# Attention in front of two expert layers: query blocks taken in pairs, and V kept in one copy

## Chip, cores and metric

One core of a Trainium2 chip runs the whole program. The metric is the device time of one execution in microseconds (us); of several executions the median is given. The engines are TensorE (PE; its weight loads are PEld), VectorE (DVE), ScalarE (ACT), GpSimd (POOL) and SyncE (SP), which here only issues DMAs.

## The reference

Four batches of eight heads, 576 tokens, head size 64, all in f32. q and k are rotated by position (rope), then attention, then a first expert layer that takes the largest of three products, then a second one in which each token goes to one of eight experts:

```
scores = (1 / sqrt(64)) * q_rot @ k_rot^T          # 4 x 8 x 576 x 576
attn   = softmax(scores)
x      = attn @ v                                  # as 2304 tokens x 512
h      = max(x @ w1, x @ w2, x @ w3)               # 512 -> 768
x      = h @ w_out                                 # 768 -> 512
e      = argmax(x @ w_gate); p = softmax(x @ w_gate)[e]
out    = p * (max(x @ W1[e], 0) @ W2[e])           # 512 -> 1024 -> 512
```

## The kernel before

**Numbers.** Most products are made of f16 pieces: each f32 operand is split into a high and a low f16 part (high = scaled value rounded, low = scaled value minus high), and three of the four products of parts are added up. Batch 0 takes its scores in f32 instead.

**Units of attention.** A batch has 36 units, made in `attention`. The tokens 0 to 511 of a batch make four query blocks c of 128 tokens (one tile of the later layers each), the last 64 tokens a fifth one. A unit (c, h) with c < 4 is one head of one query block; a unit (4, u) takes two heads of the last 64 tokens, one on each half of the partitions. The order is a list: all eight heads of block 0 (`HEADS` is 0, 2, 1, 3, 4, 6, 5, 7), then of block 1, 2, 3, then the four units of the rest. So unit 4 is the first that needs heads 4 to 7, and unit 33 the last that needs heads 0 to 3.

**A unit.** `s_part`: TensorE makes 128 x 576 scores (L636 to L656) into one of two PSUM tiles; VectorE scales them and takes their minimum (L659); ScalarE takes the exponential with its sum (L661) and writes the high part into `p16` (L663). `lo_part`: VectorE writes the low part behind it (L668), and SP issues one DMA transpose of all 128 x 1152 into `pt`, nine blocks of 128 keys (L671). `pv_part`, three units later: TensorE multiplies pt with V (L695 to L699, 14 matmuls) into columns of the one bank `o`. Block 4 of pt holds the last 64 keys of the high part and the first 64 of the low part, so the low part is shifted by 64 keys against V.

**V.** `prep_v` has two tiles per batch (heads 0 to 3 and 4 to 7): the high part `vh`, the low part `vl`, the low part of the last 64 keys `vlt`, and `v2`, the high part shifted by 64 partitions, which the low part of p is multiplied with. v2 is filled by two SBUF-to-SBUF DMAs from SP (L606, L607) and two ScalarE copies (L608, L609).

**Finish.** When all heads of a block are in the bank, `finish` multiplies it by the reciprocal sums into `x` (L729; single buffer `x32`). `transpose_x` squares x on ScalarE (L763, into the single buffer `x16`), derives a scale, writes the high part (L767) and the low part (L768) into x16, and SP issues its DMA transpose into `xT` (L772). After every second block `moe_group` queues the first expert layer for that pair of tiles: 216 matmuls of 256 columns (L799 to L801), 144 of the output product (L847 to L849), then the routing. Tiles 0 and 1 go singly; the 64-token rests of two batches make tiles 16 and 17.

**Preparation.** K and Q of the next batch come in halves of four heads: load, rope on GpSimd and VectorE, split into parts, DMA transposes into one of three buffers `kq` (L485, L486, L490). The second half of batch b + 1 takes the buffer of the first half of batch b. K, Q and V share three raw buffers, and the scales share one PSUM bank with the routing.

**Order.** Every step carries a priority (its unit's number; the first expert layer its unit's number + 22), and a list scheduler in the compiler, with its own estimate of times, fixes the order of each engine's instructions; at run time each engine takes them in that order. After attention the last tiles go through the first layer, the tokens are counted per expert, and the second layer runs slot by slot.

Of the kernel before, what the change touches and what calls it, by code (L numbers as in the profile page):

```python
# [22 lines left out]
P = 128  # L23
# [47 lines left out]
class K:  # L71
# [490 lines left out]
    def prep_v(self, b):  # L562
# [4 lines left out]
        def load():  # L567
            if b == 0:
                both = self.att.tile([P, 6, DM], F32, tag="kq0", name="vraw0", bufs=1).rearrange("p f c -> p (f c)")
            for hf in range(2):  # L570
                st["v", hf] = vp.tile([P, 56, D], F16, tag=f"v{hf}", name=f"v{hf}", bufs=1)
# [11 lines left out]
        def stats():  # L583
            sums = self.small.tile([P, 2], F32, name="v_sums")
            for hf in range(2):
                st["v2", hf] = st["v", hf][:, 32:52].rearrange("p (h r) d -> p h r d", h=4)
                nc.scalar.activation(st["v2", hf].rearrange("p a b d -> p (a b d)").bitcast(BF16),
                                     st[hf].rearrange("p a b -> p (a b)"), AF.Square, accum_out=sums[:, hf:hf + 1])
# [8 lines left out]
        def conv(hf):  # L597
            def go():
                s, x = st["s"], st[hf]
                vt, v2 = st["v", hf], st["v2", hf]  # L600
# [11 lines left out]
                self.V[b, hf] = (vh4, vl.rearrange("p (h r) d -> p h r d", r=4), v2, vt[:, 52:56])  # L612
                self.V[b, "inv"] = st["inv"]
            return go
# [3 lines left out]
    def attention(self, b):  # L618
        nc = self.nc
        steps = []  # L620
        units = [(c, h) for c in range(4) for h in HEADS] + [(4, u) for u in range(4)]
        st = {}

        def s_part(i):
            c, h = units[i]
            if c < 4 and h == 0 or c == 4 and h == 0:
# [660 lines left out]
```

## Time and profile before

| | |
|---|---|
| median of 3 runs | 927.52 us (923.73 to 932.02) |
| profiled execution | 929.0 us, span of its instructions 927.2 us |
| mean granted TensorE clock | 0.913 of full speed |
| PE, PEld, DVE, ACT, POOL busy | 84%, 69%, 72%, 62%, 27% of the span |
| attention (first score to last PV) | 22 to 604 us |
| last matmul of the first expert layer | 690 us |

Busy shares are of the whole span. PE's matmuls are pipelined and their ends are modelled, so that a busy PE is not at its peak; the clock beside it says at which part of full speed it was. A batch starts when the score of its unit 0 is read: batch 1 at 185 us, batch 2 at 330 us, batch 3 at 478 us.

### The profile page before, as it was taken

To read this page: it belongs to the slowest core of one execution; us is meant where nothing else is said; L and a number is where in the kernel's file an instruction comes from. 1 tells how busy PE (TensorE), PEld (TensorE's weight loads), DVE (VectorE), ACT (ScalarE), POOL (GpSimd) and SP (SyncE) were. 2 spreads that over 40 slices of the span, in tenths; PEclk is the share of its full clock that TensorE was granted. 3 is DMA by queue.
4 is the path that set the end of the run, shared out by engine and by line. 5 is a ranking of instruction groups with operands and counts; after the bars stand their busy time and mean duration, and the time that the engine had idled before them with its cause. 6 is when DMAs were issued, how large, how long until landed. Compare 5 with 4: busy or idle time off the path is not lost.

```text
span 927.2 us, 18852 instructions
## 1 busy us (share of the span) xinstructions
PE 782.3 (84%) x7304; PEld 641.5 (69%) x7304; DVE 670.2 (72%) x1338; ACT 574.5 (62%) x1001; POOL 249.5 (27%) x245
## 2 busy tenths in 40 slices
PE   2568899889766887879898898995899999998995
PEld 1345677677644666668677677785798889997994
DVE  6988988967796776687765687542848787765771
ACT  3677877745674765565763576521834797774772
POOL 8330003234231042131112100003312744423320
PEclk9995558999987999899989999998899999998999
DMA  8699777994999988979985799713210211133110
GB/s 250 154 218 220 194 141 118 202 176 104 157 165 136 164 140 152 143 129 150 125 132 85 106 144 128 123 39 121 107 31 30 69 47 46 44 117 137 43 36 20
DMA packets 270646, 112.24 MB, mean 121 GB/s; under 512 B 246319, under 2 KB 262847, under 8 KB 270032
## 3 DMA queue, kind: packets, MB, share of 16 engines
q1 hardware_dynamic: 260992, 81.40, 52.5%
q0 software_dynamic: 9552, 29.51, 9.9%
q8 instruction: 61, 1.00, 0.5%
q14 instruction: 41, 0.34, 0.1%
HBM read 74.97 MB, written 9.80 MB: 91 GB/s over the span
## 4 chain that ended last, share of the span: by engine, by line
PE 36%; DMA 15%; issue 4%; DVE 4%; ACT 2%; POOL 2%; SPq 0%; POOLq 0%; ACTq 0%; DVEq 0%
DMA pt<-p 7%; DMA out<-o,di 5%; PE mm L800 4%; PE mm L799 4%; PE mm L801 4%; PE pa L1201 3%; PE pa L1200 3%; PE pa L1202 3%; PE pb L1172 3%; PE pb L1170 3%; PE pb L1171 3%; PE mm L847 1%; PE mm L849 1%; DMA kq<-kls 1%; PE mm L848 1%
## 5 line engine op out<-in xcount | busy, mean ns | idle before, releaser
L799 PE MATMUL mm<-xT,w 128*128 128x256 f16 (+1 forms) x792 | 195.7, 262 | 3.1 <-DVE hm L815 2.6
L800 PE MATMUL mm<-xT,w 128*128 128x256 f16 (+1 forms) x792 | 195.7, 262 | 0.0
L801 PE MATMUL mm<-xT,w 128*128 128x256 f16 (+1 forms) x792 | 195.0, 261 | 0.0
L661 ACT ACTIVATE p<-s,bi 128x576 f32<-128x576 f32 x144 | 105.6, 734 | 82.1 <-DVE s L659 58.7
L668 DVE SCALAR_TENSOR_TENSOR p<-p,p 128x576 f16<-128x576 f32 x144 | 121.5, 846 | 26.8 <-ACT p L663 26.5
L695 PE MATMUL o<-v,pt 128*128 128x64 f16 (+1 forms) x576 | 63.0, 208 | 68.9 <-DMA pt<-p 64.8
L659 DVE TENSOR_SCALAR_CACHE_REDUCE s<-s,qk_sc 128x576 f32<-128x576 f32 x108 | 87.7, 820 | 35.2 <-PE s L646 27.7
L695 PEld LDWEIGHTS <-pt 128*128 128x128 f16 x576 | 47.7, 106 | 84.0 <-DMA pt<-p 76.7
L1109 ACT CAST h<-r 128x512 fp32r<-128x512 f32 x80 | 93.7, 1209 | 18.2 <-DMA r<-moe_w,widx 13.7
L663 ACT ACTIVATE p<-p 128x576 f16<-128x576 f32 x144 | 96.7, 679 | 6.0 <-DMA pt<-p 4.0
L1110 DVE TENSOR_TENSOR l<-r,h 128x512 fp32r<-128x512 f32 x80 | 90.1, 1165 | 5.1 <-ACT h L1109 4.6
L799 PEld LDWEIGHTS <-w 128*128 128x128 f16 x792 | 80.9, 102 | 13.3 <-DVE hm L815 2.0
L800 PEld LDWEIGHTS <-w 128*128 128x128 f16 x792 | 80.2, 101 | 11.1 <-issue 2.7
L801 PEld LDWEIGHTS <-w 128*128 128x128 f16 x792 | 80.7, 102 | 8.8 <-issue 0.7
L1200 PE MATMUL pa<-xh,h 128*128 128x256 f32 x288 | 81.5, 286 | 0.8 <-ACT xh L1131 0.8
L1201 PE MATMUL pa<-xl,h 128*128 128x256 f32 x288 | 81.6, 284 | 0.2 <-DVE xl L1132 0.2
L1202 PE MATMUL pa<-xh,l 128*128 128x256 f32 x288 | 81.6, 284 | 0.0
L847 PE MATMUL mm<-oh,h 128*128 128x256 f16 (+1 forms) x216 | 61.8, 288 | 4.8 <-DVE hm L815 3.4
L1172 PE MATMUL pb<-h,hl 128*128 128x512 f32 x152 | 61.6, 408 | 3.1 <-DVE hl L1204 3.0
L696 PE MATMUL o<-v,pt 128*128 128x64 f16 (+1 forms) x576 | 62.7, 207 | 1.1 <-DVE v L604 1.1
L1170 PE MATMUL pb<-h,hh 128*128 128x512 f32 x152 | 61.6, 408 | 0.9 <-ACT hh L1203 0.9
L927 POOL DMA_INDIRECT islot<-rows,pi x18 | 19.2, 1069 | 159.1 <-DVE pi L917 93.3
(303 smaller groups left out, 2092.4 us busy)
## 6 DMA issues: line engine op xcount, KB each, us to landing
wr<-moe_w POOLq DMA_DIRECT2D x10, 768.0 KB, 5.4
yscr<-y SPq DMA_DIRECT2D x18, 257.0 KB, 3.4
rk<-k SPq DMA_DIRECT2D x8, 512.0 KB, 5.3
vraw<-v SPq DMA_DIRECT2D x8, 512.0 KB, 5.0
rq<-q SPq DMA_DIRECT2D x7, 512.0 KB, 5.5
wr<-moe_w_out POOLq DMA_DIRECT2D x4, 768.0 KB, 6.6
pt<-p SPq DMA_TRANSPOSE x144, 3.9
v<-v SPq DMA_DIRECT2D x16, 128.0 KB, 5.3
```

The source lines that it names most:

```text
L661: nc.scalar.activation(p32, sf, AF.Exp, bias=bi, scale=-1.0, accum_out=st["sum", c][:, h:h + 1])
L663: nc.scalar.activation(p16[:, 0], p32, AF.Copy, scale=32768.0)
L668: nc.vector.scalar_tensor_tensor(out=p16[:, 1], in0=p32, scalar=32768.0, in1=p16[:, 0], op0=ALU.mult, op1=ALU.subtract)
L695: nc.tensor.matmul(out, lhsT=pt[:, blk], rhs=sel(vh, blk), start=blk == 0, stop=False)
L799: nc.tensor.matmul(pv[:, i], lhsT=wh, rhs=xT[:, k, :n], start=k == 0, stop=False)
L800: nc.tensor.matmul(pv[:, i], lhsT=wh, rhs=xT[:, 4 + k, :n], start=False, stop=False)
L801: nc.tensor.matmul(pv[:, i], lhsT=wl, rhs=xT[:, k, :n], start=False, stop=k == 3)
L1109: nc.scalar.copy(T["h1"][:, :, j], r[:, :, j])
L1110: nc.vector.tensor_tensor(out=T["l1"][:, :, j], in0=r[:, :, j], in1=T["h1"][:, :, j].bitcast(F32), op=ALU.subtract)
L1200: nc.tensor.matmul(ps[:, i], lhsT=h1[:, k, j + i], rhs=xh[:, k], start=k == 0, stop=False)
L1201: nc.tensor.matmul(ps[:, i], lhsT=h1[:, k, j + i], rhs=xl[:, k], start=False, stop=False)
L1202: nc.tensor.matmul(ps[:, i], lhsT=l1[:, k, j + i], rhs=xh[:, k], start=False, stop=k == 3)
```

## The change

Four things change together; the functions they touch are `prep_v`, `attention` and `finish`.

- From batch 1 on, units go by pairs of query blocks: heads 0 to 3 of blocks 0 and 1, then heads 4 to 7 of both; heads 0 to 3 of blocks 2 and 3, then the two units of the rest with these heads; heads 4 to 7 of blocks 2 and 3, then the other two units of the rest. Batch 0 keeps blocks 0 and 1 as they are. Heads 4 to 7 are first needed at unit 8, heads 0 to 3 last at unit 25.
- Each group of eight units (two of the rest) fills the bank `o` and is finished by itself: half of two tiles at a time. x holds two tiles (`x32` is twice as wide), and both are transposed, one after the other, when the second half is done.
- In p16 the low part's last 64 keys come right behind the high part's, and the other 512 after them. So the low part is written in two operations of 64 and 512 columns, and its blocks lie like V's: the first five blocks of pt take the high and the low part of V, the other four the high part again.
- V has no shifted copy: one ScalarE copy and one VectorE operation over all 20 columns blocks, no DMAs; the low part's rows for the second 64 partitions of the last block are set to zero.

```diff
@@ prep_v, conv @@
-                vh, vl, vlt = vt[:, 0:16], vt[:, 16:32], vt[0:64, 52:56]
-                nc.gpsimd.memset(vt[64:128, 52:56], 0.0)
-                nc.scalar.activation(vh, x[:, 0:16], AF.Copy, scale=s)
-                nc.vector.scalar_tensor_tensor(out=vl, in0=x[:, 0:16], scalar=s, in1=vh, op0=ALU.mult, op1=ALU.subtract)
-                vh4 = vh.rearrange("p (h r) d -> p h r d", r=4)
-                nc.sync.dma_start(v2[0:64, :, 1:5], vh4[64:128])
-                nc.sync.dma_start(v2[64:128, :, 0:4], vh4[0:64])
-                nc.scalar.activation(v2[0:64, :, 0], x[0:64, 16:20], AF.Copy, scale=s[0:64])
-                nc.scalar.activation(v2[64:128, :, 4], x[64:128, 16:20], AF.Copy, scale=s[64:128])
-                nc.vector.scalar_tensor_tensor(out=vlt, in0=x[0:64, 16:20], scalar=s[0:64], in1=v2[0:64, :, 0],
-                                               op0=ALU.mult, op1=ALU.subtract)
+                nc.scalar.activation(vt[:, 0:20], x, AF.Copy, scale=s)
+                nc.vector.scalar_tensor_tensor(out=vt[:, 20:40], in0=x, scalar=s, in1=vt[:, 0:20], op0=ALU.mult, op1=ALU.subtract)
+                nc.gpsimd.memset(vt[64:128, 36:40], 0.0)
@@ attention @@
-        units = [(c, h) for c in range(4) for h in HEADS] + [(4, u) for u in range(4)]
+        two = lambda p, hf: [(c, h) for c in (2 * p, 2 * p + 1) for h in HEADS[4 * hf:4 * hf + 4]]
+        rest = lambda hf: [(4, 2 * hf), (4, 2 * hf + 1)]
+        first = [[(c, h) for h in HEADS] for c in range(2)] if b == 0 else [two(0, 0), two(0, 1)]
+        groups = first + [two(1, 0), rest(0), two(1, 1), rest(1)]
+        units = [u for g in groups for u in g]
@@ lo_part @@
-            nc.vector.scalar_tensor_tensor(out=p16[:, 1], in0=p32, scalar=32768.0, in1=p16[:, 0],
-                                           op0=ALU.mult, op1=ALU.subtract)
+            for o, i0, n in ((S, 512, 64), (S + 64, 0, 512)):
+                nc.vector.scalar_tensor_tensor(out=p16[:, o:o + n], in0=p32[:, i0:i0 + n], scalar=32768.0,
+                                               in1=p16[:, i0:i0 + n], op0=ALU.mult, op1=ALU.subtract)
@@ pv_part @@
+            for blk in range(5):
+                for a in range(2):
+                    nc.tensor.matmul(out, lhsT=pt[:, blk], rhs=sel(a, blk), start=blk + a == 0, stop=False)
             for blk in range(4):
-                nc.tensor.matmul(out, lhsT=pt[:, blk], rhs=sel(vh, blk), start=blk == 0, stop=False)
-                nc.tensor.matmul(out, lhsT=pt[:, blk], rhs=sel(vl, blk), start=False, stop=False)
-            for blk in range(5):
-                nc.tensor.matmul(out, lhsT=pt[:, 4 + blk], rhs=sel(v2, blk), start=False, stop=False)
-            nc.tensor.matmul(out, lhsT=pt[:, 4], rhs=last(), start=False, stop=True)
+                nc.tensor.matmul(out, lhsT=pt[:, 5 + blk], rhs=sel(0, blk), start=False, stop=blk == 3)
@@ finish, blocks 2 and 3 of batch 0 and all of later batches @@
+        elif c < 4:
+            if hf == 0:
+                self.x2 = self.pw.tile([P, 2, DM], F32, tag="x32", name="x32", bufs=1)
+            x = self.x2
+            nc.vector.tensor_tensor(out=x[:, :, 256 * hf:256 * hf + 256].rearrange("p c (h d) -> p c h d", d=D),
+                                    in0=o_ps.rearrange("p (c h d) -> p c h d", c=2, d=D),
+                                    in1=r.rearrange("p (c h) -> p c h", c=2).unsqueeze(3).to_broadcast([P, 2, 4, D]), op=ALU.mult)
+            if hf:
+                pair = [4 * b + c - 1, 4 * b + c]
+                for i, t in enumerate(pair):
+                    self.X[t] = (x[:, i], vinv)
+                    self.transpose_x(t)
+                self.moe_group(pair)
```

## Rows read from the trace of the kernel before

**Rows 1.** The page's first part: busy us, share of the span, instructions of each engine.

```profile
PE 782.3 (84%) x7304; PEld 641.5 (69%) x7304; DVE 670.2 (72%) x1338; ACT 574.5 (62%) x1001; POOL 249.5 (27%) x245
```

**Rows 2.** Busy time by stage: PE, PEld, DVE, ACT, POOL; granted clock, DMA share, GB/s.

```profile
200.00:220.00 20.00, 17.03 (x182) 13.84 (x180) 11.27 (x24) 4.70 (x11) 12.72 (x11) 0.91 0.62 132
260.00:300.00 40.00, 24.74 (x262) 17.44 (x260) 30.28 (x73) 24.67 (x51) 9.06 (x8) 0.74 1.02 154
...
345.00:357.00 12.00, 11.39 (x108) 9.26 (x109) 8.89 (x23) 5.94 (x14) 4.08 (x4) 0.86 0.59 109
480.00:505.00 25.00, 21.98 (x243) 18.54 (x242) 15.45 (x26) 10.73 (x22) 6.33 (x6) 0.93 0.78 124
604.00:640.00 36.00, 35.33 (x328) 31.18 (x326) 15.90 (x69) 8.02 (x16) 4.24 (x6) 1.00 0.09 23
...
300.00:600.00 300.00, 257.82 (x3094) 206.91 (x3092) 216.31 (x501) 182.12 (x374) 49.89 (x49) 0.95 0.86 132
```

**Rows 3.** The same for L800 alone (PE, PEld; granted clock, DMA share, GB/s).

```profile
265.30:282.70 17.40, 0.00 (x0) 0.00 (x0) 0.66 0.91 159
```

**Rows 4.** TensorE's waits (us, times, longest): whole run, 185 to 604, 480 to 604.

```profile
PE o L695 <- DMA pt<-p: 64.8, 45, 6.0
...
PE o L695 <- DMA pt<-p: 54.0, 39, 6.0
PE o L695 <- DVE w L752: 2.2, 1, 2.2
...
PE o L695 <- DMA pt<-p: 10.7, 8, 3.8
```

**Rows 5.** Timeline, VectorE: scores of units 3, 4, 8 (batch 1), 4, 8 (2, 3).

```profile
193.76 0.83 DVE L659 TENSOR_SCALAR_CACHE_REDUCE s<-s,qk_sc 128x576 f32<-128x576 f32 x1 [0.60 <-PE s L646]
...
220.02 0.83 DVE L659 TENSOR_SCALAR_CACHE_REDUCE s<-s,qk_sc 128x576 f32<-128x576 f32 x1 [0.49 <-PE s L646]
...
232.92 0.81 DVE L659 TENSOR_SCALAR_CACHE_REDUCE s<-s,qk_sc 128x576 f32<-128x576 f32 x1
...
356.93 0.83 DVE L659 TENSOR_SCALAR_CACHE_REDUCE s<-s,qk_sc 128x576 f32<-128x576 f32 x1 [2.04 <-PE s L646]
...
372.78 0.82 DVE L659 TENSOR_SCALAR_CACHE_REDUCE s<-s,qk_sc 128x576 f32<-128x576 f32 x1 [4.56 <-PE s L646]
...
505.57 0.83 DVE L659 TENSOR_SCALAR_CACHE_REDUCE s<-s,qk_sc 128x576 f32<-128x576 f32 x1 [3.32 <-PE s L646]
...
515.82 0.83 DVE L659 TENSOR_SCALAR_CACHE_REDUCE s<-s,qk_sc 128x576 f32<-128x576 f32 x1 [0.38 <-PE s L646]
```

**Rows 6.** Timeline of SP's issues (last Q transpose; V copies), and an issue-to-landing row.

```profile
173.60 0.62 SPq L606 DMA_DIRECT2D v<-v  x1
...
177.15 1.36 SPq L671 DMA_TRANSPOSE pt<-p  x1
...
213.78 2.73 SPq L490 DMA_TRANSPOSE kq<-qs  x1
...
kq<-qs SPq DMA_TRANSPOSE x6, 5.5
```

**Rows 7.** Timeline of tile 5's passage (square, transpose issue), and us to landing.

```profile
267.44 0.61 ACT L763 ACTIVATE x<-x 128x512 bf16<-128x512 f32 x1
...
277.75 1.23 SPq L772 DMA_TRANSPOSE xT<-x  x1
...
xT<-x SPq DMA_TRANSPOSE x18, 3.3
```

**Rows 8.** VectorE: L668 (ns min/median/max), and four 128-column operations in a row.

```profile
L668 DVE SCALAR_TENSOR_TENSOR p<-p,p x144: 702/752/3180, 32.0 to 598.2; 128x576 f16<-128x576 f32 x144
...
198.21 0.99 DVE L752 TENSOR_TENSOR w<-o,r 64x128 f32<-64x128 f32 x4
```

**Rows 9.** Timeline: last two x transposes on SP; TensorE reaches tiles 14, 15.

```profile
600.50 8.24 SPq L772 DMA_TRANSPOSE xT<-x  x2
...
615.53 0.27 PE L799 MATMUL mm<-xT,w 128*128 128x256 f16 x1
```

More of the change, by code (lines that the diff above doesn't have):

```diff
@@ L570, in load @@
             for hf in range(2):
-                st["v", hf] = vp.tile([P, 56, D], F16, tag=f"v{hf}", name=f"v{hf}", bufs=1)
+                st["v", hf] = vp.tile([P, 40, D], F16, tag=f"v{hf}", name=f"v{hf}", bufs=1)
                 if b == 0:
@@ L620, in attention, with place @@
         steps = []
-        units = [(c, h) for c in range(4) for h in HEADS] + [(4, u) for u in range(4)]
-        st = {}
+        two = lambda p, hf: [(c, h) for c in (2 * p, 2 * p + 1) for h in HEADS[4 * hf:4 * hf + 4]]
[3 more added lines that the diff above has]
+        units = [u for g in groups for u in g]
+        where = [(n, k, len(g)) for n, g in enumerate(groups) for k in range(len(g))]
+        st = {}
+        def place(i):
+            c, h = units[i]
+            if c == 4:
+                return h % 2
+            return h if b == 0 and c < 2 else 4 * (c % 2) + h % 4
         def s_part(i):
             c, h = units[i]
-            if c < 4 and h == 0 or c == 4 and h == 0:
-                st["sum", c] = self.small.tile([P, 8], F32, tag="sums", name="sums", bufs=3)
+            n, k, _ = where[i]
+            if k == 0:
+                st["sum", n] = self.small.tile([P, 8], F32, tag="sums", name="sums", bufs=3)
             ps = self.s_ps.tile([P, 2, 512], F32, tag="s", name="s")
@@ L676, in pv_part @@
             pt = st.pop(i)
-            if h == 0:
-                st["o", c] = self.o_ps.tile([P, 512], F32, tag="o", name="o")
-                r = self.small.tile([P, 8], F32, tag="r", name="r")
-                st["r", c] = r
-            o_ps = st["o", c]
+            n, k, size = where[i]
+            if k == 0:
+                st["o", n] = self.o_ps.tile([P, 512], F32, tag="o", name="o")
+                st["r", n] = self.small.tile([P, 8], F32, tag="r", name="r")
+            o_ps, at = st["o", n], place(i)
@@ L682, in pv_part @@
             if c < 4:
                 hf, hh = divmod(h, 4)
-                vh, vl, v2, vlt = self.V[b, hf]
-                out = o_ps[:, 64 * h:64 * h + 64]
-                sel = lambda t, blk: t[:, hh, blk]
-                last = lambda: vlt[:, hh]
+                vt = self.V[b, hf].rearrange("p (a x) d -> p a x d", a=2)
+                out = o_ps[:, 64 * at:64 * at + 64]
+                sel = lambda a, blk: vt[:, a, 4 * hh + blk if blk < 4 else 16 + hh]
             else:
                 hf, j = divmod(h, 2)
-                vh, vl, v2, vlt = self.V[b, hf]
@@ L703, in attention @@
+            for blk in range(4):
+                nc.tensor.matmul(out, lhsT=pt[:, 5 + blk], rhs=sel(0, blk), start=False, stop=blk == 3)
+            if k == size - 1:
+                self.finish(b, c, hf, st, n)
         for i in range(len(units) + LAG):
@@ L717, in attention, with finish @@
         return steps
-    def finish(self, b, c, st):
+    def finish(self, b, c, hf, st, g):
         nc = self.nc
-        o_ps, sums = st.pop(("o", c)), st.pop(("sum", c))
-        n = 8 if c < 4 else 4
-        r = st.pop(("r", c))
+        o_ps, sums, r = st.pop(("o", g)), st.pop(("sum", g)), st.pop(("r", g))
+        n = 8 if c < 4 else 2
         nc.vector.tensor_scalar(out=r[:, :n], in0=sums[:, :n], scalar1=1e-9, scalar2=None, op0=ALU.add)
@@ L747, in finish @@
+            x = self.X[16 + i][0]
             x3 = x.rearrange("p (a o j d) -> p a o j d", a=2, o=2, j=2)
-            o4 = o_ps.rearrange("p (a j d) -> p a j d", a=2, j=2)
+            o4 = o_ps[:, :256].rearrange("p (j d) -> p j d", j=2)
             for o in range(2):
                 pi = slice(64 * o, 64 * o + 64)
-                for a in range(2):
-                    nc.vector.tensor_tensor(out=x3[pr, a, o], in0=o4[pi, a, :, 64 * o:64 * o + 64],
-                                            in1=r[pi, 2 * a:2 * a + 2].unsqueeze(2).to_broadcast([64, 2, D]), op=ALU.mult)
@@ L754, in finish @@
-            if b % 2:
+                nc.vector.tensor_tensor(out=x3[pr, hf, o], in0=o4[pi, :, 64 * o:64 * o + 64],
+                                        in1=r[pi, 0:2].unsqueeze(2).to_broadcast([64, 2, D]), op=ALU.mult)
+            if b % 2 and hf:
                 self.transpose_x(16 + i)
```

50 lines of the change are left out of this document (22 added, 28 removed).

## The prediction

> **What bounds the kernel now.** I read the page's engine shares and slices first, then a table by stage, then the waits of TensorE, then single instructions. TensorE is the busiest engine at 84% [rows 1]; no other reaches three quarters of the span. The reader is to see in the stage table that this share is two regimes. After the last attention unit, from 604 to 640 us, it is busy 35.33 of 36 us at full clock; between 300 and 600 us, with attention running, 257.82 of 300 at a granted clock of 0.95 [rows 2]. So TensorE bounds the time from the first batch to the last expert tile, and the only thing to win there is its idle time and its low-clock time. Attention is not a chain whose length sets the end: first-MoE matmuls wait behind it in first-come order and fill its gaps, and what it doesn't let in comes after it.
>
> The waits say where the idle time is: 64.8 us in 45 waits of the PV matmul for its transposed probabilities pt [rows 4]. They hurt most between 260 and 300 us, where TensorE works 24.74 of 40 us at clock 0.74 [rows 2]. The reason stands in the windows of the first-MoE line: from 265.3 to 282.7 it has no matmul at all [rows 3]. The pair of tiles 2, 3 was used up and tile 5 was not transposed yet (its transpose is issued at 277.75 [rows 7]), so nothing filled the waits. I call this the hole. Its price: the usual rate is 257.82/300 x 0.95 = 0.816 of full speed, here it is 24.74/40 x 0.74 = 0.458; 40 us x 0.358 = 14.3 us of work, which at 0.816 take 17.5 us.
>
> The hole has a cause further up. In batch 1 the score of unit 3 reaches VectorE at 193.76 and that of unit 4 at 220.02 [rows 5]. Unit 4 is the first with heads 4 to 7, and their last transpose is issued at 213.78 and lands some 5.5 us later [rows 6]. The same step costs less in batch 2 (unit 4 at 356.93) and batch 3 (505.57). Meanwhile TensorE eats the MoE backlog.
>
> **The change part by part.** The sum is made against the profiled execution: 929.0 us, span 927.2, so 1.8 lie around it; it is 1.5 above the median of 927.5.
>
> *The order of units.* In batches 1 to 3 heads 4 to 7 are first needed at unit 8, not 4. If their K and Q are ready when they are now, unit 8 starts where unit 4 starts now: 232.92 - 220.02 = 12.9 us earlier, then 372.78 - 356.93 = 15.9, then 515.82 - 505.57 = 10.3 [rows 5]; 39 us of attention time altogether. Most of it isn't a gain, because TensorE works during these stalls: idle only 2.97 of 20, 0.61 of 12 and 3.02 of 25 us in the three stretches [rows 2]. What gains is this:
> (a) The hole. Tile 5 comes 12.9 us earlier. Against that, both tiles of a pair now finish in one step, and the second goes through the single x16 buffer after the first. One such passage ran from the square at 267.44 over the transpose issue at 277.75 to its landing some 3.3 us later, 13.6 us [rows 7]; at the end of attention, where the engines are freer, the second of two issues comes 8.24 - 1.3 = 7 us after the first [rows 9]. Between 7 and 13.6 I take 7, because there too two passages follow directly on each other, which leaves 12.9 - 7 = 6 us. One microsecond of hole costs about one (17.5 for 17.4). Ends: 0 and 12.9.
> (b) First-MoE work moved from the stalls behind attention. The stalls run at (17.03 + 11.39 + 21.98)/57 of the time and a mean clock of 0.908, together 0.803 of full speed; the tail at 35.33/36 = 0.981. 39 us x 0.803 = 31.3 us of work, 31.9 us in the tail: gain 7.1. I take 5, because other waits may slide into the denser attention; ends 0 and 7.1.
> The K buffer that heads 4 to 7 of the next batch take is read for the last time at unit 25 instead of 33; this brings nothing as long as unit 8 finds them ready, and counts 0.
>
> *No shifted copy of V.* Sixteen copies leave SP's queue. The four for batch 1 keep SP from 173.60 to 177.15, and a pt transpose stands right behind them [rows 6]. All 16 at some 0.62 us are 10 us of SP, most of it beside other work; for this one group I count 3 us, ends 0 and 10. Two ScalarE copies and one VectorE operation per half of V go too and the remaining ones get a quarter wider: some 1 us per half, on engines with a quarter of their time free, counted 0; if that cover were gone it would be 8 us of gain.
>
> *The low part in two operations.* Per unit VectorE gets 512 + 64 columns for 576: 144 more instructions. The 576-column one takes 0.752 us at the median, and four 128-column operations in a row take 0.99 us, 0.25 each [rows 8]. So the extra one costs less than 0.25, 36 us in all at most, on an engine that is busy 216.31 of 300 us [rows 2]. On the path it can only matter where TensorE waits for pt: 45 waits x 0.25 = 11 us at most, nothing at least. I take 3, as the compiler's order can put PV later.
>
> *One more hand-over of the o bank.* Six groups of PV per batch for five, with one PSUM bank: the next group's first PV stands in TensorE's queue until VectorE has read the bank, and all matmuls behind it wait too. The one such wait on record is 2.2 us [rows 4]; four more hand-overs are 0 to 8.8 us, I take 2. The PV itself stays 14 matmuls.
>
> *The last pair.* Tiles 14 and 15 are ready two units later than now, plus the second passage. Now the transpose of tile 15 is issued at 600.50 and TensorE reaches the pair at 615.53 [rows 9], a cover of 11.7 us after landing. With attention up to 39 us earlier the cover grows: 0. Without that shift the lack would be some 2 x 3 + 7 - 11.7 = 1 us.
>
> The transposes of x that move: seven first tiles of a pair go 8 to 10 units later on SP and ScalarE, past the pt transposes between; no one needs them before the second tile.
>
> Sum: -6 - 5 - 3 + 3 + 2 = -9, so 920.0 against 929.0, and 918.5 against the median; I say 918.
>
> **The rivals.** *More than the hole.* Batch 3, which prepares no next batch, waits for pt 10.7 us in all; batches 1 and 2 share 54.0 - 10.7 = 43.3 [rows 4]. If the lighter queues take half of the difference of 43.3 to 2 x 10.7, 11 us, and the hole closes for 12.9, the sum is -9 - 11 - 7 = -27: 900. For it speaks that v copies stood ahead of pt; against it that the K and Q transposes, which stay, are longer (2.73 us of SP each [rows 6]).
>
> *The stall only moves.* The preparation of heads 4 to 7 shares three raw buffers and one PSUM bank with V; if the compiler's order puts it later because unit 8 is later, unit 8 waits as unit 4 did. Then (a) and (b) vanish: -3 + 3 + 2 = +2, 930 on the median. Against it: its start isn't tied to the units that use it but to buffers.
>
> *The clock.* The hole shows it: with only attention to do, TensorE had a mean granted clock of 0.66 for 17 us, part of them at 2.4 and part at 1.2 GHz [rows 3]. With first-MoE work moved out, more stretches could look so. If batches 2 and 3, some 235 us, lost 0.04 of clock out of 0.95, that is 10 us, 928. The rule behind it stands in the Trainium skill, TensorE: Matmul & The Clock Gate, section "HAM oscillation — how this bites in real kernels": gaps on the PE drop the gate to half rate. By it moving filler out of attention speaks against this change; the rows at 265 us agree for a stretch without any filler, none shows what a thinner filler does.
>
> *Slower: the pair's passage stops ScalarE.* The square of the second tile writes the same x16 that the first one's transpose is still reading. ScalarE takes its work in order, so if the square is queued too early, the exponentials of the next units, and with them pt and TensorE, stand behind it. And x2 is one buffer: VectorE's product for the next first half waits until both passages of the pair are done, holding the o bank. One landing is 3.3 us [rows 7] after an issue of 1.3; seven pairs x 4.6 = 32 us on ScalarE, half of it exposed is 16, and (a) is lost: -9 + 16 + 6 = +13, 941 on the median. It decides from some 9/7 = 1.3 us of exposed wait per pair. For it: two passages of 13.6 us make 27, about as long as the eight units to the next first half. Against it: the compiler's order knows the buffers.
>
> **How the numbers follow.** Forecast 0.50 (909 to 927 by the bounds of its terms), more than the hole 0.16, stall only moves 0.11, clock 0.06, slower 0.17. A kernel of this time is told from no change at about 1%, below 918.2 or above 936.8. Half of the forecast and all of the first rival lie below: 0.25 + 0.16, about 0.42; slower is the last rival, with a little of the two before it left out: 0.17; the rest 0.41. The range for 8 in 10 reaches from the first rival to the last, cutting both: 899 to 938.
>
> **What would show it.** The score of unit 4 in batches 1 to 3 follows unit 3 within 6 us, and the gap at unit 8 is under 10. The last PV lies 30 to 40 us before 604. No stretch of 10 us between 180 and 600 without first-MoE matmuls; clock in 260 to 300 above 0.85. VectorE has 144 more operations and 14 to 36 us more work; SP has no v copies. Waits for pt stay at 50 to 70 us. The prediction is wrong if ScalarE waits more than 1 us before squares, if a hole stays, or if TensorE's waits for pt grow by over 10 us.

## The result and the profile after

The changed kernel takes 939.8 us (median of 4 runs, 936.3 to 944.8), the kernel before, run beside it, 928.9 (923.7 to 932.0): ratio 1.0115, 95% interval 1.0069 to 1.0161. Executions more than 1.5% above the fastest of the same kernel are left out of the ratios, here and below. The forecast was 918, with a range of 899 to 938. The profiled execution of the changed kernel took 940.4 us, its span 938.6.

The page's first part, with VectorE's 144 operations more (x1482 against x1338) and 12.5 us more of its work [rows 1]; then the stage table, for the stretches of [rows 2], and L810 (L800 before) in its hole [rows 3]:

```profile
PE 791.1 (84%) x7304; PEld 647.0 (69%) x7304; DVE 682.7 (73%) x1482; ACT 570.3 (61%) x985; POOL 239.2 (25%) x245
```

```profile
260.00:300.00 40.00, 32.49 (x386) 24.78 (x385) 37.79 (x86) 27.84 (x60) 11.55 (x9) 0.89 0.70 134
300.00:600.00 300.00, 253.08 (x3031) 202.49 (x3030) 224.22 (x592) 180.47 (x366) 49.54 (x54) 0.94 0.87 132
604.00:640.00 36.00, 32.56 (x307) 28.74 (x308) 14.12 (x55) 8.63 (x19) 1.17 (x2) 1.00 0.13 31
...
290.60:297.50 6.90, 0.00 (x0) 0.00 (x0) 0.67 0.68 126
```

The bad stretch of before is repaired: TensorE works 32.49 of 40 us between 260 and 300 for 24.74, at clock 0.89 for 0.74, and the hole is 6.9 us long for 17.4. The end is 11 us later all the same. TensorE's waits for pt in the whole run are 70.1 us in 50 times for 64.8 in 45 [rows 4], at the edge of the 50 to 70 that were expected. Now the scores at VectorE (start, length; units 3, 4, 7, 8 of batch 1, then 7 and 8 of batches 2 and 3), against [rows 5]:

```profile
204.84 0.82 DVE L661 TENSOR_SCALAR_CACHE_REDUCE s<-s,qk_sc 128x576 f32<-128x576 f32 x1 [3.82 <-PE s L648]
208.70 0.83 DVE L661 TENSOR_SCALAR_CACHE_REDUCE s<-s,qk_sc 128x576 f32<-128x576 f32 x1
220.87 0.81 DVE L661 TENSOR_SCALAR_CACHE_REDUCE s<-s,qk_sc 128x576 f32<-128x576 f32 x1
231.37 0.82 DVE L661 TENSOR_SCALAR_CACHE_REDUCE s<-s,qk_sc 128x576 f32<-128x576 f32 x1 [0.91 <-PE s L648]
354.24 0.82 DVE L661 TENSOR_SCALAR_CACHE_REDUCE s<-s,qk_sc 128x576 f32<-128x576 f32 x1
371.49 0.82 DVE L661 TENSOR_SCALAR_CACHE_REDUCE s<-s,qk_sc 128x576 f32<-128x576 f32 x1 [1.18 <-PE s L648]
503.78 0.81 DVE L661 TENSOR_SCALAR_CACHE_REDUCE s<-s,qk_sc 128x576 f32<-128x576 f32 x1
511.18 0.83 DVE L661 TENSOR_SCALAR_CACHE_REDUCE s<-s,qk_sc 128x576 f32<-128x576 f32 x1 [3.07 <-PE s L648]
```

Unit 4 no longer waits (3.9 us after unit 3, 26.3 before). But now unit 8 does: 10.5, 17.25 and 7.4 us after unit 7. It comes 1.5, 1.3 and 4.6 us earlier than before, not 12.9, 15.9 and 10.3. Its last transposition and what that hung on (SP, then GpSimd, then SP; beside [rows 6]):

```profile
199.84 3.24 SPq L486 DMA_TRANSPOSE kq<-kls  x1
...
204.55 1.26 POOL L405 TENSOR_TENSOR t<-rq,rope 128x512 f32<-128x512 f32 x1 [9.64 <-DMA kq<-kls]
...
225.14 2.81 SPq L490 DMA_TRANSPOSE kq<-qs  x1
```

The rotation of Q writes the same single tile (t2) that holds the low part of K until its transposition has landed. GpSimd stood 9.64 us for it, and Q's transposition went out at 225.14, 11.4 us later than before. Tile 5's transposition, the end of the hole, is the second line here; before it was at 277.75 [rows 7]. The third line is TensorE's last matmul for tile 1 in the first expert layer; before, the same matmul (L849) started at 208.79:

```profile
283.87 1.33 SPq L782 DMA_TRANSPOSE xT<-x  x1
294.38 1.23 SPq L782 DMA_TRANSPOSE xT<-x  x1
...
224.29 0.43 PE L859 MATMUL mm<-oh,h 128*128 128x264 f16 x1
```

So the hole closed from its left end: the work ahead of it was late (pair 2, 3 ended at 290.5, 25.3 later than before), and the tile that ends it came 16.6 us later. From there to the last matmul of the first layer (704.4) the changed kernel needs 480.1 us; the kernel before needs 481.2 from 208.8 to 690.0. By this mark the loss lies before 225 us, and everything that was to be gained after it is absent.

### The profile page after: what moved, and what is told of

It reads as the page before. It is cut to its first block, busy times and chain, and to the rows that moved or that the text cites. A ratio compares the mean times of both kernels' runs of the same rounds, so it can differ in the third digit from the quotient of the medians.

```text
span 938.6 us, 19032 instructions
## 1 busy us (share of the span) xinstructions
PE 791.1 (84%) x7304; PEld 647.0 (69%) x7304; DVE 682.7 (73%) x1482; ACT 570.3 (61%) x985; POOL 239.2 (25%) x245
## 4 chain that ended last, share of the span: by engine, by line
PE 35%; DMA 24%; DVE 15%; issue 13%; ACT 8%; POOL 3%; SPq 2%; POOLq 0%; DVEq 0%; ACTq 0%
DMA pt<-p 11%; PE pa L1211 3%; PE mm L809 3%; PE pa L1210 3%; PE pa L1212 3%; DVE p L671 3%; DVE s L661 3%; PE mm L810 3%; PE mm L811 3%; PE pb L1182 2%; PE pb L1180 2%; DMA vraw<-v 2%; PE pb L1181 2%; DMA xT<-x 2%; PE o L698 2%
## 5 line engine op out<-in xcount | busy, mean ns | idle before, releaser
L810 PE MATMUL mm<-xT,w 128*128 128x256 f16 (+1 forms) x792 | 196.9, 263 | 0.0
L663 ACT ACTIVATE p<-s,bi 128x576 f32<-128x576 f32 x144 | 106.0, 736 | 73.0 <-DVE s L661 56.8
L698 PE MATMUL o<-v,pt 128*128 128x64 f16 (+1 forms) x1440 | 82.1, 210 | 72.0 <-DMA pt<-p 70.1
L671 DVE SCALAR_TENSOR_TENSOR p<-p,p 128x64 f16<-128x64 f32 (+1 forms) x288 | 133.9, 506 | 11.7 <-ACT p L665 11.2
L698 PEld LDWEIGHTS <-pt 128*128 128x128 f16 x1440 | 68.4, 107 | 87.5 <-DMA pt<-p 84.1
L1119 ACT CAST h<-r 128x512 fp32r<-128x512 f32 x80 | 93.2, 1197 | 19.6 <-DMA r<-moe_w,widx 14.4
L810 PEld LDWEIGHTS <-w 128*128 128x128 f16 x792 | 81.2, 103 | 11.1 <-issue 2.8
L857 PE MATMUL mm<-oh,h 128*128 128x256 f16 (+1 forms) x216 | 61.6, 287 | 6.5 <-DVE hm L825 5.1
L638 PE MATMUL s<-kq 64*128 64x512 f32 (+1 forms) x72 | 60.3, 990 | 7.5 <-ACT p L663 7.5
L859 PE MATMUL mm<-oh,h 128*128 128x256 f16 (+1 forms) x216 | 60.6, 287 | 4.9 <-DVE h L839 2.7
```

The costliest lines, as they stand in the source:

```text
L663: nc.scalar.activation(p32, sf, AF.Exp, bias=bi, scale=-1.0, accum_out=st["sum", n][:, place(i):place(i) + 1])
L671: nc.vector.scalar_tensor_tensor(out=p16[:, o:o + n], in0=p32[:, i0:i0 + n], scalar=32768.0, in1=p16[:, i0:i0 + n], op0=ALU.mult, op1=ALU. ...
L698: nc.tensor.matmul(out, lhsT=pt[:, blk], rhs=sel(a, blk), start=blk + a == 0, stop=False)
L810: nc.tensor.matmul(pv[:, i], lhsT=wh, rhs=xT[:, 4 + k, :n], start=False, stop=False)
L1119: nc.scalar.copy(T["h1"][:, :, j], r[:, :, j])
```

## The experiments

Ratios are to the kernel before, run beside each of the five groups below (929.8, 946.7, 929.2, 930.7 and 927.3 us; the second group ran on a slower chip).

**First group: the parts by themselves.** Theory A: the extra VectorE operations cost. Theory B: the pair's passage through x16 stops ScalarE (the prediction's slower rival). Theory C: the fixed order's own scatter. The order alone was not run: the wider x32 takes the memory that V's copy gives up.

v_only, the old order with V and the low part as in the change:

```diff
@@ conv, lo_part and pv_part as in the change; for instance @@
-                nc.sync.dma_start(v2[0:64, :, 1:5], vh4[64:128])
-                nc.sync.dma_start(v2[64:128, :, 0:4], vh4[0:64])
+                nc.scalar.activation(vt[:, 0:20], x, AF.Copy, scale=s)
@@ kept @@
         units = [(c, h) for c in range(4) for h in HEADS] + [(4, u) for u in range(4)]
```

> Before's order of units and its finish, with the changed kernel's V (no shifted copy) and its low part in two operations. Theory A (the 144 extra VectorE operations cost what was lost, above all in batch 0 where VectorE is busiest): 8 to 13 us slower than before. Theory B (the pair's two passages through one x16 buffer stop ScalarE and TensorE): no slower than before, 4 us faster to 2 slower, as there are no pairs of passages here. Theory C (a new static order scatters the time by 1% whatever is changed): anywhere within 10 us of before.

937.13 us, 1.0068 (1.0032 to 1.0105).

split_only, the kernel before with the low part in two operations:

```diff
+            for i0, n in ((512, 64), (0, 512)):
+                nc.vector.scalar_tensor_tensor(out=p16[:, 1, i0:i0 + n], in0=p32[:, i0:i0 + n], scalar=32768.0,
+                                               in1=p16[:, 0, i0:i0 + n], op0=ALU.mult, op1=ALU.subtract)
```

> The kernel before, only with the low part of p written in two VectorE operations of 64 and 512 columns into the same places; V's copies stay. Theory A: 8 to 13 us slower than before. Theory B: 0 to 3 us slower. Theory C: anywhere within 10 us.

934.92, 1.0059 (1.0031 to 1.0087). Both lie between the ranges of A and B, and inside C's.

after_onelow, the changed kernel with one low operation (the low products stand beside the wrong rows of V):

```diff
-            for o, i0, n in ((S, 512, 64), (S + 64, 0, 512)):
+            nc.vector.scalar_tensor_tensor(out=p16[:, S:], in0=p32, scalar=32768.0, in1=p16[:, :S],
+                                           op0=ALU.mult, op1=ALU.subtract)
```

> The changed kernel with the low part in one operation of 576 columns; the low parts of the keys then stand beside the wrong rows of V, so the small low-part products are wrong, and all else is as it was. Theory A: 8 to 13 us faster than the changed kernel, so at the time of before or up to 4 us below. Theory B: 0 to 3 us faster than the changed kernel, still 8 to 11 above before.

931.74, 1.0021 (0.9993 to 1.0049).

after_x16, the changed kernel with two buffers x16:

```diff
-tag="x16", name="x16", bufs=1)
+tag="x16", name="x16", bufs=2)
```

> The changed kernel with two x16 buffers, so that the square of a pair's second tile need not wait for the first one's transpose. Theory B: ScalarE's 15.7 us of waits for xT vanish and the kernel is 6 to 12 us faster than the changed one. Theory A: within 4 us of the changed kernel, 7 to 12 above before.

941.14, 1.0114 (1.0067 to 1.0160). ScalarE's wait for xT, 15.7 us in 8 times in the changed kernel, is gone from its list of waits; the time is not. So nothing speaks for theory B. Theory A looked confirmed by after_onelow: one operation less, 0.9% back.

**Second group: the fourth corner, and doses.** v_onelow is v_only with the edit of after_onelow; three_b0 and three_b13 are the kernel before with three low operations in batch 0 or in the others; after_pool gives the 64 columns to GpSimd:

```diff
@@ three_b0 (three_b13: b > 0) @@
+            for i0, n in ((512, 64), (0, 256), (256, 256)) if b == 0 else ((0, S),):
@@ after_pool @@
+            t = p32[:, 512:S]
+            nc.gpsimd.tensor_scalar(out=t, in0=t, scalar1=32768.0, scalar2=None, op0=ALU.mult)
+            nc.gpsimd.tensor_tensor(out=p16[:, S:S + 64], in0=t, in1=p16[:, 512:S], op=ALU.subtract)
```

> The old order of units with no shifted copy of V, and the low part of p made in one VectorE operation of 576 columns as before (so the low products stand beside the wrong rows of V: that part of the output is changed). With it the four corners of order by number of low operations are all run without copies: old and new order, one operation and two. If the four V copies of each batch were worth what the prediction took for them (term (c), -3 us, down to -10), this kernel comes to 920 to 927 where the kernel before has 929.8. If the copies were hidden anyway it is 929 to 932, and the split alone then makes 937.1 of it (the old order without copies with two low operations). The order's own worth is the new order with one low operation (931.7 in the call before) less this kernel: theory 'the order is worth its hole' (the prediction's (a) and (b), -11) wants this kernel at 940 or more, theory 'the hole was filled by work that came later by as much' wants it within 3 us of 931.7.

1.0069 (1.0031 to 1.0106): without the two operations nothing comes back.

> The kernel before, with the low part in three VectorE operations (64, 256 and 256 columns) in batch 0 alone: 72 operations more, all in the first 185 us, where VectorE was 96 to 99% busy in several stretches. Copies and order as before. Theory 'place' (an extra operation costs its whole length where VectorE has no slack, batch 0, and next to nothing later): twice the cost of the split's 36 operations there; if all of the 5.5 us that the split cost in the old order arose in batch 0, this is 929.8 + 11 = 941, and the same kernel with the extra operations in the other batches stays at 930. Theory 'share' (each extra operation costs the same wherever it is): 5.5 us for 144 operations gives 0.038 us each, 72 of them 2.8 us, 932.5, and the other kernel 929.8 + 8.2 = 938.

1.0066 (1.0024 to 1.0109).

> The kernel before, with the low part in three VectorE operations (64, 256 and 256 columns) in batches 1 to 3 alone: 216 operations more between 185 and 600 us, where VectorE is about 71% busy. Theory 'place': 930 to 932, since VectorE has room there and TensorE's filler work covers the rest. Theory 'share': 929.8 + 216 x 0.038 = 938.

1.0150 (1.0096 to 1.0205). Per added operation 0.09 and 0.07 us: 'share', not 'place', and twice the price of split_only's.

> The changed kernel with the 64-column low part on GpSimd (a multiplication in place and a subtraction) in place of VectorE's second operation; the result is the same. VectorE then has 144 operations as before, each of 512 columns, some 0.1 us shorter than the 576-column one. Theory 'VectorE's room' (the split costs because VectorE has no slack): the time falls from 940 to that of the changed kernel with one low operation, 931.7, or a little under it (928 to 932). Theory 'length of the chain' (the split costs because the transposition comes later by one operation): GpSimd's two operations take longer than VectorE's one, so the transposition comes later still and the time stays at 938 to 945. Against both: GpSimd is 58% busy in the first 60 us with the preparation of keys and queries, and a tail queued behind one of those operations would hold up the units of batch 0; then PV's waits on the transposed tile grow above all there.

1.0292 (1.0241 to 1.0343). The operations of the low part by shape (busy, mean ns, idle time before), then a wait of ScalarE (us, times, longest):

```profile
L671 POOL TENSOR_SCALAR p<-p 128x64 f32<-128x64 f32 x144 | 84.0, 586 | 186.5 <-ACT p L665 148.1 <-issue 34.6 <-DVE w L332 2.7
L672 POOL TENSOR_TENSOR p<-p,p 128x64 f16<-128x64 f32 x144 | 61.8, 434 | 8.1
L673 DVE SCALAR_TENSOR_TENSOR p<-p,p 128x512 f16<-128x512 f32 x144 | 120.6, 843 | 38.7 <-issue 18.0 <-ACT p L665 17.8 <-POOL p L672 1.9
...
ACT p L663 <- POOL p L672: 32.9, 10, 9.5
```

GpSimd's two take 1.02 us where VectorE's one took 0.32, and ScalarE's exponential (L663) stood 32.9 us for the second of them. VectorE was lightened, to 120.6 us on the low part from the 133.9 of the changed kernel, but the chain grew longer and got a new wait, so the test doesn't tell the theories apart. What does speak is the square of order and operations without copies: old order 1.0069 with one, 1.0068 with two; new order 1.0021 with one, 1.0115 with two. The split costs nothing in one order and 0.9% in the other, so no sum of parts holds, unless the order of instructions moves the time by as much, which the controls below show.

**Third group: the stall, and controls.** after_kls and v_kls give the low part of K a tile of its own once the weights' buffers are closed; n_shift and after_shift change a priority, and no instruction:

```diff
-            kls = self.raws.tile([P, 18, 2, D], F16, tag="t2", name="kls", bufs=1)
+            pool, tag = (self.vp[1], "kls") if len(self.vp) > 1 else (self.raws, "t2")
+            kls = pool.tile([P, 18, 2, D], F16, tag=tag, name="kls", bufs=1)
@@ n_shift, after_shift @@
-MOE_SHIFT = 22
+MOE_SHIFT = 21.5
```

> The changed kernel with a tile of its own for the low part of K (kls) in batches 2 and 3 and the second half of batch 1, where it had shared the one tile t2 with the rotation of Q. In the changed kernel the rotation of Q for heads 4 to 7 of batch 1 began at 204.55, when the transposition of kls issued at 199.84 had landed, though its raw Q was there from about 183; Q's transposition was issued at 225.14 and unit 8's score was read at 231.37, 10.5 after unit 7's (17.25 in batch 2, 7.4 in batch 3: 35 in all). Theory 'the stall moved' (the wait went from unit 4 to unit 8 because the chain of preparation hangs on the shared tile, not on the buffer of the keys, and it is what the change still pays for): the rotation starts up to 18 us earlier, the three gaps shrink by 20 or more, and the time falls by 10 us or more against the changed kernel, to a ratio of 1.002 or less against the kernel before. Theory 'the work decides' (VectorE's extra operations and TensorE's own work set the pace, and the gaps at unit 8 are covered by the first expert layer's matmuls): the gaps shrink and the ratio stays at 1.008 to 1.014.

940.34, 1.0111 (1.0067 to 1.0156). Q's transposition for unit 8 and the scores of units 7 and 8 of batches 1, 2 and 3:

```profile
211.68 3.10 SPq L491 DMA_TRANSPOSE kq<-qs  x1
...
228.60 0.82 DVE L662 TENSOR_SCALAR_CACHE_REDUCE s<-s,qk_sc 128x576 f32<-128x576 f32 x1
230.07 0.82 DVE L662 TENSOR_SCALAR_CACHE_REDUCE s<-s,qk_sc 128x576 f32<-128x576 f32 x1
358.95 0.81 DVE L662 TENSOR_SCALAR_CACHE_REDUCE s<-s,qk_sc 128x576 f32<-128x576 f32 x1
360.89 0.83 DVE L662 TENSOR_SCALAR_CACHE_REDUCE s<-s,qk_sc 128x576 f32<-128x576 f32 x1 [0.46 <-PE s L649]
501.81 0.82 DVE L662 TENSOR_SCALAR_CACHE_REDUCE s<-s,qk_sc 128x576 f32<-128x576 f32 x1
505.68 0.83 DVE L662 TENSOR_SCALAR_CACHE_REDUCE s<-s,qk_sc 128x576 f32<-128x576 f32 x1 [0.91 <-PE s L649]
```

The gaps are 1.5, 1.9 and 3.9 us for 35 in all, and the first layer's hole is 1.4 us (297.9 to 299.3). The time is that of the changed kernel, and the last PV is not earlier: 608.1 us, for 605.4. That the shared tile makes the stall is shown; the 10 us that theory 'the stall moved' expected from its end did not come.

> The old order of units without copies of V, low part in two operations (1.0068 times the kernel before), with the same tile of its own for the low part of K. In the kernel before, Q's transposition for unit 4 of batch 1 was issued at 213.78, and the rotation of Q ahead of it began at 201.98, after the transposition of kls issued at 196.11. Theory 'the stall moved': the same shared tile makes the stall of unit 4, so the gaps at unit 4 (26.3 in batch 1) shrink by 10 to 15 each without any change of order, and the hole of the first expert layer with them; the ratio falls to 0.99 to 1.00. Theory 'the work decides': the gaps shrink and the ratio stays at 1.004 to 1.010.

933.59, 1.0053 (1.0022 to 1.0084), against 1.0068 without the tile. The gaps at unit 4 shrank to 2.2, 8.2 and 3.5 us from the 18.4, 15.3 and 16.4 of v_only: the same tile makes the old order's stall too, and there too its end brought next to nothing.

> A control: the kernel before with the first expert layer's priority 21.5 units behind its tile in place of 22. Every instruction is the same, only the fixed order in which the engines take them differs (about a third of TensorE's). Theory 'scatter' (any edit that re-deals the fixed order costs some tenths of a per cent, and the differences of the half edits are of that size): the ratio lies 0.3% or more from 1, as 1.003 to 1.008. Theory 'cost' (the half edits' differences are their own): 0.998 to 1.002.

0.9988 (0.9942 to 1.0034). This rests on five of twelve executions; the median of all twelve is 935.0 us, 1.006 of the 929.2 beside it, so the control doesn't show that the order is free.

> The same control on the changed kernel: the first expert layer's priority 21.5 units behind its tile in place of 22, every instruction the same (about a third of TensorE's in another order). Theory 'cost': 1.0095 to 1.0135, as the changed kernel itself (1.0115, 1.0114 with a second x16). Theory 'scatter': 0.3% or more away from 1.0115, on either side.

950.64, 1.0242 (1.0207 to 1.0277): the instructions of the changed kernel in another order, 1.3% slower than it. Theory C, so far held to be small, is larger than what was to be explained.

**Fourth group: where, and what the memory can buy.** after_one_b0 and after_one_b13 have one low operation in batch 0, or in batches 1 to 3 (low products beside the wrong rows of V there). mix keeps the old order, with V's copies and one operation in batches 0 and 2 and without copies in 1 and 3; mix_kls adds K's own tile:

```diff
@@ after_one_b0 (after_one_b13: b > 0) @@
+            for o, i0, n in ((S, 0, S),) if b == 0 else ((S, 512, 64), (S + 64, 0, 512)):
@@ mix, mix_kls: prep_v; pv_part and lo_part likewise @@
+        return self.prep_v_new(b) if b % 2 else self.prep_v_old(b)
```

> The changed kernel with the low part in one operation in batch 0 alone (36 operations fewer; there the low products stand beside the wrong rows of V), two operations in batches 1 to 3. Theory 'batch 0' (all of the extra operations' cost arises where VectorE has no slack, the first 200 us): the second product of tile 1 ends at 209 to 214 in place of 224, and the ratio is 1.000 to 1.004, as with one operation everywhere (1.0021). Theory 'everywhere' (36 of 144 operations are a quarter of the 0.94%): 1.008 to 1.011.

938.00, 1.0086 (1.0049 to 1.0124): tile 1's mark came at 214, as theory 'batch 0' had it, the time did not.

> The other part: the changed kernel with one low operation in batches 1 to 3 (108 operations fewer; there the low products stand beside the wrong rows of V) and two in batch 0. Theory 'batch 0': 1.009 to 1.013, no better than the changed kernel, and the second product of tile 1 still ends at 220 or later. Theory 'everywhere': three quarters of the 0.94% back, 1.003 to 1.006.

947.59, 1.0190 (1.0130 to 1.0250): 108 operations fewer than the changed kernel, and slower. Both theories on the operations' place fall.

> The old order; batches 0 and 2 with the copies of V and one low operation as before, batches 1 and 3 without copies and with two operations, and with the memory that this frees a tile of its own for the low part of K (batches 2, 3 and the second half of batch 1). Its result is the reference's. Theory 'batch 0': the first 209 us as before, then the 472 us that the old order with its own tile for K's low part took from the second product of tile 1 to the end of the first layer, against 481: 9 us less than the kernel before, a ratio of 0.988 to 0.994. Theory 'work decides / scatter': 0.998 to 1.006.

917.11 (915.25 to 924.41), 0.9866 (0.9817 to 0.9915): faster than both kernels, with the two parts near what 'batch 0' had named (209.0 and 468.6 us).

> The same as the kernel with mixed layouts, but with the low part of K in the shared tile as before: what the own tile does by itself in the kernel beside it. Theory 'batch 0': between 0.998 and 1.003 (54 fewer copies-and-operations in no place that decides), so that the own tile is worth 0.6% or more. Theory 'everywhere': 72 of 144 extra operations, half of the 0.59 to 0.68% of the half edits, 1.003.

935.75, 1.0060 (1.0026 to 1.0093).

**Fifth group: two more controls.** before_ahead is the kernel before, mix_kls_shift the faster one, each with one priority moved:

```diff
@@ before_ahead @@
-PREP_AHEAD, PREP_STEP = (20, 20, 20), 0.3
+PREP_AHEAD, PREP_STEP = (26, 26, 26), 0.3
@@ mix_kls_shift @@
-MOE_SHIFT = 22
+MOE_SHIFT = 21.5
```

> A second control on the kernel before: the preparation of the next batch has a priority of 26 units ahead of its batch in place of 20; every instruction the same, some 29% of TensorE's in another order. Theory 'scatter': 0.4% or more away from 1, on either side. Theory 'cost': 0.997 to 1.003, as the first control (0.9988).

938.15, 1.0107 (1.0059 to 1.0156).

> A control on the faster kernel: the kernel of mixed layouts with the own tile for K's low part, with the first expert layer's priority 21.5 units behind its tile in place of 22; every instruction the same, in another order. If the own tile is what gains, this stays at 0.982 to 0.993 (0.9866 before). If that was a lucky order, it comes back to 0.997 to 1.008, to the range of the kernels without the tile.

939.09, 1.0105 (1.0053 to 1.0157): 2.4% slower than the same instructions in the other order.

Where the order puts the time can be read from the stretch between 210 us and the end of the first layer, in which the same work is left to all but for some matmuls. TensorE's busy time and its waits for pt there, of the kernel before and of before_ahead, mix_kls, mix_kls_shift, the changed kernel and after_shift, in this order:

```profile
210.00:690.00 480.00, 402.44 (x4601) 327.70 (x4600) 330.72 (x770) 271.39 (x536) 98.15 (x92) 0.93 0.75 124
...
PE o L695 <- DMA pt<-p: 50.5, 35, 6.0
```

```profile
210.00:705.30 495.30, 399.76 (x4577) 326.45 (x4575) 329.27 (x766) 268.77 (x533) 99.01 (x90) 0.93 0.76 121
...
PE o L695 <- DMA pt<-p: 63.3, 35, 6.1
```

```profile
210.00:677.60 467.60, 396.07 (x4616) 324.55 (x4613) 323.61 (x831) 267.80 (x531) 87.36 (x86) 0.93 0.76 126
...
PE o L747 <- DMA pt<-p: 35.7, 26, 5.0
PE o L764 <- DMA pt<-p: 14.1, 7, 6.3
```

```profile
210.00:697.00 487.00, 399.12 (x4618) 327.12 (x4616) 328.22 (x831) 269.10 (x531) 91.02 (x87) 0.93 0.73 122
...
PE o L747 <- DMA pt<-p: 34.1, 20, 6.4
PE o L764 <- DMA pt<-p: 19.7, 12, 4.9
```

```profile
210.00:704.40 494.40, 411.10 (x4695) 335.56 (x4691) 345.32 (x884) 273.76 (x538) 95.03 (x95) 0.93 0.73 121
...
PE o L698 <- DMA pt<-p: 53.0, 39, 5.2
```

```profile
210.00:713.40 503.40, 410.53 (x4696) 334.58 (x4693) 343.10 (x890) 271.90 (x537) 101.24 (x96) 0.92 0.75 119
...
PE o L698 <- DMA pt<-p: 59.5, 30, 6.6
```

Within a pair of equal instructions the number of matmuls (x4601 and x4577, x4616 and x4618, x4695 and x4696) and TensorE's busy time agree within 3.1 us, the clock within 0.01; the stretch differs by 15.3, 19.4 and 9.0 us. It is idle time, 18.0, 16.4 and 9.6 us of it. Waits for pt are 12.8 us of the first and 6.5 of the third, but only 4.0 of the second, where the rest is spread over others. Between the two kernels of the change it is another thing: 94 matmuls and 8.7 us of TensorE more are left over at 210, and the rest, 14.4 - 8.7 = 5.7 us, is idle.

These left-over matmuls are lost late. Up to 150 us the kernel before had made 654 matmuls and the changed one 647; from 150 to 210, before and after:

```profile
150.00:210.00 60.00, 51.07 (x697) 42.49 (x695) 49.60 (x108) 41.31 (x84) 19.96 (x19) 0.97 0.88 157
150.00:210.00 60.00, 50.22 (x612) 40.77 (x611) 50.53 (x119) 40.41 (x78) 21.02 (x19) 0.89 0.86 145
```

TensorE is busy nearly as long and makes 85 matmuls fewer, of a somewhat different mix of shapes, at a granted clock of 0.89 for 0.97. That is an estimated 60 x 0.08 = 4.8 us of full-speed time, over half of the 8.7. The clock is thus a rival for the loss in this part that no run tests. It is not enough by itself, as split_only had 0.89 there too and is not late.

The two parts of the profiled executions, in us (to the start of the last matmul of tile 1's second product, and from there to that of the first layer; the second group, on the slower chip, and n_shift are left out). Each figure is from one execution, and executions of one kernel differ by 11 us and more (v_only, 930.8 to 942.3):

| kernel | batch 0: low operations, copies | first part | rest |
|---|---|---|---|
| before, before_ahead | one, copies | 208.8, 206.8 | 481.2, 498.5 |
| mix, mix_kls, mix_kls_shift | one, copies | 204.8, 209.0, 211.0 | 488.8, 468.6, 486.0 |
| split_only | two, copies | 208.1 | 489.1 |
| after_onelow, after_one_b0 | one, no copies | 212.8, 214.0 | 479.0, 486.9 |
| after, after_x16, after_kls | two, no copies | 224.3, 222.0, 224.5 | 480.1, 482.2, 483.4 |
| after_shift, after_one_b13 | two, no copies | 218.0, 222.9 | 495.4, 496.0 |
| v_only, v_kls | two, no copies | 225.6, 224.7 | 479.8, 472.1 |

All seven kernels with two operations and no copies in batch 0 are late by the end of tile 1, at 218 to 226; the eight others are there at 205 to 214. The rest runs from 469 to 499 and follows no part of the change: the new order stands at 479 to 496, the old one at 469 to 499.

## Why the prediction was wrong

**The step that failed first** is the assumption under the order of units: "If their K and Q are ready when they are now, unit 8 starts where unit 4 starts now". They were not ready: the preparation hangs on the shared tile t2, and the wait moved to unit 8, which came 1.5, 1.3 and 4.6 us earlier for the 12.9, 15.9 and 10.3 of the forecast. The mechanism of the rival "the stall only moves" happened, on another buffer than it named. Terms (a) and (b) had nothing left to stand on: the last PV went from 603.45 to 605.35, not 30 to 40 us forward.

**The price of the stall**, 11 us in (a) and (b), did not show either. after_kls has the stall and the hole all but closed, 7.3 us of gaps for 35 and a hole of 1.4 us for 17.4, and neither its attention nor its time is shorter than the changed kernel's. A gain of up to a per cent could hide behind a worse order of instructions (see below), but none is seen.

**(a), the hole.** It became 10.5 us shorter, where 6 were taken with an upper end of 12.9, but not by the step that was forecast: tile 5 came 16.6 us later, not earlier, and the hole closed by late work ahead of it. Here a microsecond less of hole was no gain, because its right end did not come earlier.

**The small terms** (no shifted copy of V, -3; the low part in two operations, +3; the o bank, +2) can't be sized but for the last: the changed kernel has no wait of PV for VectorE's reading of the bank, for the one of 2.2 us before. The low part had an upper end of 11; the half edits give 5.5 (split_only), nothing (old order without copies) and 9 (new order). The bound of 0.25 us for the further operation was right: VectorE spends 133.9 us on the low part for 121.5, 0.09 us more per unit. The mean durations, 319 ns for 64 columns and 694 for 512 against 846 for 576, don't add up to that, because the second operation starts 137 ns after the first (median), before the first one's end. The Trainium skill, Vector Engine (DVE) Microarchitecture Reference, section "5.2 Measured stream behaviour on trn2 (trn3 not measured)", gives some 75 ns for each further instruction after overlap; this trace agrees with its 0.09 us. The copies of V were to be a gain, and v_onelow, which does nothing but take them out, is 0.7% slower, itself no more than a re-dealt order can make.

**What the sum left out** is the largest effect of all: the list scheduler deals the order anew for an edit, and the prediction allowed that only as a reason inside small terms. Equal instructions in other orders moved the time by -0.1 (+0.6 by all executions) and +1.1% (kernel before), +1.3% (changed kernel) and +2.4% (mix_kls). A change of +1.15% is inside that. In two of the three pairs above most of the lost time is in the wait that the prediction read first, TensorE's for pt; in mix_kls and its control it is a quarter. The Trainium skill, PSUM — Partial Sum Buffer, section "Engine vs sequencer instructions", states that matmuls start in program order. The runs agree with it as far as they go: with equal work in another order, 50.5 us of these waits became 63.3. That other matmuls stood ready behind them is not shown.

**The rivals.** The slower one came out at 941, next to the measured 939.8, and that is luck: ScalarE's waits before squares are there, and after_x16 took 15.7 us of them away for nothing. The clock was 0.94 for 0.95 between 300 and 600, no cause there; the rule cited for it spoke against thinning the filler, and the stretch without filler became shorter. Between 150 and 210, a stretch that the prediction did not price, the clock was lower.

**What stays open** is what makes the changed kernel 1.15% slower. Two operations and missing copies together, and neither alone, go with some 10 to 15 us in the first 210; whether by their cost, by an order that the scheduler deals for such a batch 0, or by the clock that TensorE then has, no run tells. It is open, too, whether the changed kernel's order of units is better or worse than the old one by less than a per cent; for gains of that size after_x16 and after_kls are no proof either. And how much of mix_kls's 1.3% is its own tile: its re-deal lost all of it, so it is a faster kernel, not a shown mechanism.

## What to carry to other kernels

Where a scheduler fixes the order, first move one priority by a little and time that: an effect within its spread, here 1 to 2%, can't be put down to a single edit, and the spread belongs in the range. A hole in the filler is a gain only if what ends it comes earlier; ask of a removed wait which shared buffer makes the next one. Half edits that don't add up may be the sign of a re-dealt order; test that before explaining an interaction. And durations of operations that overlap are not to be added up: take the busy time of the group.

## What the hardware showed beside it

GpSimd's 128x64 operations took 586 and 434 ns in the mean where VectorE's one took 319. VectorE's 512-column operation beside them went from 694 to 843 ns in the mean, but only from 683 to 693 in the median: the rest is in a few long ones, up to 3.1 us, and the kernel before has such ones as well (median 752, mean 846, longest 3180 ns [rows 8]). The clock of the first 64 us is shown as 1.00 in the kernel before, yet its f32 score matmuls of 512 columns took 2.07 us for two at 51.75 and 0.84 at 62.55: both of TensorE's levels, 1.2 and 2.4 GHz, lie under one figure, so mean clocks of whole runs (0.88 to 0.95 here) are not to be compared. These are the two rows:

```profile
51.75 2.07 PE L636 MATMUL s<-kq 64*128 64x512 f32 x2 [0.82 <-ACT p L661]
...
62.55 0.84 PE L636 MATMUL s<-kq 64*128 64x512 f32 x2
```
